# Issuing the zero fills behind the weight loads, with one wait on the output weight

## The chip, the cores and the metric

One Trainium2 chip, one of its cores. The metric is the time of one execution on the device, in microseconds (us). Of the core's engines, PE multiplies matrices, DVE and ACT work on vectors, and SP, ACT and POOL issue DMAs, the copies between memories that 16 DMA engines carry out. "Chain of compute" means the operations that wait for one another from the first load to the last store; a DMA "lands" when its completion is signalled. Executions fall into groups: most take about 766.7 us, others about 783 or 800 us. An execution more than 1.5% above the fastest of its kernel is called slow here, the rest fast.

## The reference

It is one decode step of attention with a feed-forward gate, forward and backward. What matters here is the outputs' size. The caches of keys and values have 2 batches, 8 heads, 32,768 positions and 128 channels, but attention only sees the last 4,096 positions:

```python
W = min(4096, max(256, Sk // 4))                     # 4096 of Sk = 32768
k = jnp.repeat(k_cache[:, :, Sk - W:, :], rep, axis=1)
v = jnp.repeat(v_cache[:, :, Sk - W:, :], rep, axis=1)
...
_out, _vjp = jax.vjp(_f, A_x, A_k_cache, A_v_cache, A_wq, ...)
_grads = _vjp(grad_out)                              # gradients of both whole caches
```

So the gradients of both caches are whole caches (`out_2`, `out_3`), zero in the first 28,672 positions of each of 2 × 16 parts. One part's zeros are 7.34 MB, all of them 235 MB. The rest is small in bytes: weights, 33.6 MB of cache read, 33.6 MB of gradient written.

## The kernel before

The zeros are written from one small tile, by DMAs that POOL issues (`zf`). A "row" is the stretch of bytes that a DMA moves in one piece, for the zeros as it stands in the output. Five parts are cut into several DMAs. The others go out as one DMA each, with rows of 28,672 bytes, or of 57,344 bytes for the 13 parts listed in `zlong`:

```python
def zf(o, q, r0, nent, rows, rep=1):
    ...
    w = rows * DH
    if w > ZG * DH:                  # ZG = 112: a row of 112 * 128 bf16 is 28,672 bytes
        v = v.bitcast(F32)           # 14,336 x f32: 57,344 bytes
        w //= 2
    ...
    sw_fill.append(nc.gpsimd.dma_start(out=v, in_=zs))

zlong = (3, 5, 7, 11, 12, 16, 17, 18, 19, 22, 23, 24, 28)
zshort = {2: (...), 4: (...), 6: (...), 8: (...), 10: (...)}
for qi in range(ZQ - 1):                       # 31 parts, 47 DMAs, right at the start
    r = 0
    whole = (P, ZR // P, 1) if qi in zlong else (P, ZG, ZR // (P * ZG))
    for n, rows, rep in zshort.get(qi, (whole,)):
        r = zf(*zparts[qi], r, n, rows, rep)
```

Further down come the loads. The small ones are issued by ACT, the weights and caches by SP. The LayerNorm and all that follows it need `b2` first in this program's order, then `w1`, `w2`, then `wo`:

```python
dma_store.dma_start(out=b2_bf[:], in_=B_b2...)       # ACT's queue, 1 KB
dma_load.dma_start(out=w1, ...)                      # SP's queue, 1.8 MB
dma_load.dma_start(out=w2, ...)                      # 1.8 MB
dma_load.dma_start(out=wo[:], ...)                   # 4.2 MB
dma_load.dma_start(out=wq[:], ...)                   # 4.2 MB
vnat = load(A_v_cache, 0, "v")                       # 4.2 MB
... # LayerNorm, feed-forward, transposes of wo, w1, w2
knat = load(A_k_cache, 0, "k")                       # reuses the buffer of w1 and w2
... # four rounds of attention: load, compute, store 4.2 MB each of keys and values
... # epilogue
last = nc.sync.dma_start(out=out_6..., in_=dw1_st[:])
with tc.issue_after(last.ins):
    fin = nc.sync.dma_start(out=v, in_=zs)           # zeros of the 32nd part, last of SP
tc.add_manual_dep(fin.ins, sw_fill[-2].ins.name, ...)   # once POOL's second-to-last zero DMA has landed
... # gradient of wo, its store
```

## Time and profile before

| | before |
|---|---|
| time, median of the first 6 runs | 766.78 us (fast runs 766.68 to 766.83) |
| bytes moved | 326.73 MB |
| profiled run | slow: span 797.6 us |
| `wo` lands after its issue | 37.5 us |
| `b2` (1 KB) lands after its issue | 31.2 us |

The page divides the span into 40 equal slices. In the DMA line each digit is the busy share of the 16 DMA engines in tenths, 9 meaning 90% or more; under it stands what they moved. From the page of the kernel before (a slow run: its end is not typical):

```profile
DMA  9999999999999999999999999999999999994089
GB/s 355 437 425 426 436 429 436 421 440 417 434 431 429 433 442 416 434 429 433 434 435 437 429 420 430 432 437 443 422 423 434 434 445 417 429 436 179 1 368 394
```

The engines are busy in all slices but two near the end. Slices 2 to 36 average 431 GB/s, and 326.73 MB at 431 GB/s are 758 us: the fast time of 766.7 us is little more than the bytes. The Trainium skill, "HBM Reference", section "Specifications (TRN2)", gives about 425 GB/s for a core that streams alone, bounded by its 16 DMA engines; this trace agrees, with 431 GB/s.

The timeline of the kernel before shows the start. Columns: start, duration, engine, line, operation, count, and in brackets the idle time before it and what ended it.

```profile
1.64 0.50 SPq L227 DMA_DIRECT2D wo<-in_A_wo_dram  x1
...
4.92 5.20 POOL L101 DMA_DIRECT2D out_dram<-zt  x8 [3.26 <-DVE zt L81]
...
33.20 0.17 DVE L242 CAST b2T<-b_bf 128x4 f32<-128x4 bf16 x1 [18.51 <-DMA b_bf<-in_B_b_dram]
...
33.49 1.87 PE L162 MATMUL pp<-xT_f,ones_f 128*128 128x2 f32 x8 [24.56 <-DVE goT L238]
...
43.68 0.61 POOL L101 DMA_DIRECT2D out_dram<-zt  x1 [33.57 <-DMA out_dram<-zt]
```

POOL issues eight zero DMAs at once, and the ninth at 43.68 us, when the first has landed: at most eight are in flight, called the ring below. The first LayerNorm matmul waits for a copy that stands behind the copy of `b2`, which comes at 33.2 us.

In windows (length, then busy time of PE, weight load, DVE, ACT and POOL, then granted clock, DMA share and GB/s), the first 10 us are the other stretch below the plateau:

```profile
0.00:5.00 5.00, 0.29 (x4) 0.20 (x4) 3.39 (x4) 1.28 (x1) 1.16 (x9) 1.00 0.62 213
5.00:10.00 5.00, 0.26 (x4) 0.28 (x4) 3.24 (x10) 0.00 (x0) 5.00 (x8) 1.00 1.02 345
...
39.00:46.00 7.00, 4.76 (x82) 4.55 (x83) 1.84 (x5) 0.71 (x1) 0.61 (x1) 1.00 1.01 430
```

The issues of the kernel before, with the median time to landing in the last column. In the key and value lines it is not a median of four: asked load by load, the profile gives a landing for the third value load alone, and for the second and fourth key loads.

```profile
nat<-in_A_v_cache_dram SPq DMA_DIRECT2D x4, 4096.0 KB, 33.3
nat<-in_A_k_cache_dram SPq DMA_DIRECT2D x4, 4096.0 KB, 38.7
...
wo<-in_A_wo_dram SPq DMA_DIRECT2D x1, 4096.0 KB, 37.5
```

### The profile page before, as it was taken

The numbers are of one execution on the slowest core, as the hardware profiler recorded it, in microseconds if no ns is written. First come the engines' busy times: TensorE is split into PE (matmuls) and PEld (weight loads), VectorE is DVE, ScalarE is ACT, GpSimd is POOL, SyncE is SP. The second block draws the span as 40 slices with busy tenths as digits, with TensorE's granted clock in tenths as the row PEclk, the third lists the DMA queues.
The fourth block names the chain that finished last, engine by engine and source line by source line (L and its number), as shares of the span: only waits on it lengthen the run. The fifth ranks groups of instructions, "written<-read, shape, count | busy, mean of one in ns | idle before, by whom it ended". The sixth has DMA issues, their size and how long they took to land.

```text
span 797.6 us, 9402 instructions
## 1 busy us (share of the span) xinstructions
PE 412.2 (52%) x4118; PEld 268.4 (34%) x4118; DVE 276.8 (35%) x484; ACT 214.8 (27%) x313; POOL 30.2 (4%) x56
## 2 busy tenths in 40 slices
PE   0265772747503757760573578102608587275690
PEld 0253362634103645420353443002507343134230
DVE  3034241355401436440141375100304555113770
ACT  0024531145400234550120256100202456120260
POOL 3000000010000100000000000000000000000000
PEclk9998897868756995675595968655958577556555
DMA  9999999999999999999999999999999999994089
GB/s 355 437 425 426 436 429 436 421 440 417 434 431 429 433 442 416 434 429 433 434 435 437 429 420 430 432 437 443 422 423 434 434 445 417 429 436 179 1 368 394
DMA packets 12473, 326.73 MB, mean 410 GB/s; under 512 B 2276, under 2 KB 2284, under 8 KB 2294
## 3 DMA queue, kind: packets, MB, share of 16 engines
q0 software_dynamic: 8000, 227.55, 67.5%
q1 hardware_dynamic: 2696, 56.63, 20.3%
q10 hardware_dynamic: 1736, 41.95, 12.4%
q8 instruction: 32, 0.52, 0.2%
q14 instruction: 9, 0.07, 0.0%
HBM read 45.62 MB, written 280.50 MB: 409 GB/s over the span
## 4 chain that ended last, share of the span: by engine, by line
DMA 38%; PE 31%; DVE 14%; ACT 7%; issue 4%; another core or an unknown queue 3%; ACTq 0%; DVEq 0%; SPq 0%
DMA out_dram<-nat 14%; DMA nat<-in_A_k_cache_dram 10%; DMA nat<-in_A_v_cache_dram 9%; PE ov L410 5%; PE tp L377 4%; PE s_ps L383 4%; DMA b_bf<-in_B_b_dram 4%; DVE tT L156 3%; PE dp_ps L383 2%; DVE ds_bf L457 2%; ACT p_bf L444 2%; DVE nat L156 2%; PE wps L628 2%; ACT tT L154 2%
## 5 line engine op out<-in xcount | busy, mean ns | idle before, releaser
L377 PE MATMUL tp<-pperm,nat 128*128 128x128 bf16 x1024 | 84.8, 234 | 177.7 <-DMA nat<-in_A_v_cache_dram 123.6
L156 DVE COPY tT<-tp 128x1024 bf16<-128x1024 bf16 x96 | 64.0, 689 | 244.1 <-PE tp L377 243.7
L377 PEld LDWEIGHTS <-nat 128*128 128x128 bf16 x1024 | 74.0, 106 | 184.1 <-DMA nat<-in_A_v_cache_dram 125.3
L154 ACT COPY tT<-tp 128x1024 bf16<-128x1024 bf16 x32 | 32.4, 1012 | 307.2 <-PE tp L377 307.2
L154 ACT CAST nat<-ov 128x512 bf16<-128x512 f32 x160 | 87.9, 589 | 58.3 <-PE ov L410 57.0
L156 DVE CAST nat<-ov 128x512 bf16<-128x512 f32 x96 | 65.3, 690 | 54.0 <-PE ov L410 53.0
L410 PE MATMUL ov<-bd,ds_bf 128*128 128x512 bf16 x128 | 50.6, 473 | 5.9 <-DVE nat L156 3.9
L410 PE MATMUL ov<-bd,p_bf 128*128 128x512 bf16 x128 | 48.7, 449 | 4.6 <-DVE nat L156 1.8
L383 PE MATMUL dp_ps<-tT,zdo 128*128 128x256 bf16 x256 | 41.1, 293 | 15.2 <-DVE tT L156 8.9
L101 POOL DMA_DIRECT2D out_dram<-zt x47 | 28.6, 613 | 524.3 <-DMA out_dram<-zt 521.0
L383 PE MATMUL s_ps<-tT,zq 128*128 128x256 bf16 x256 | 39.4, 280 | 14.8 <-DVE tT L156 8.8
L383 PEld LDWEIGHTS <-zdo 128*128 128x128 bf16 x256 | 25.5, 104 | 23.3 <-issue 19.9
L399 PE MATMUL ps<-t,nat 128*128 128x16 bf16 x1024 | 28.5, 173 | 7.8 <-DVE bd L367 7.8
L399 PEld LDWEIGHTS <-nat 128*128 128x128 bf16 x1024 | 28.5, 103 | 11.0 <-issue 5.8
L383 PEld LDWEIGHTS <-zq 128*128 128x128 bf16 x256 | 24.8, 100 | 22.0 <-issue 19.5
L495 PE MATMUL wps<-dq_rows,xn_bf 2*128 2x512 bf16 x32 | 14.5, 521 | 22.9 <-ACT wq L154 17.7
L391 PE MATMUL tp<-ident_bf,p_bf 128*128 128x128 bf16 x64 | 7.5, 311 | 34.9 <-ACT p_bf L444 34.9
L444 ACT ACTIVATE p_bf<-e_sb,rl 32x512 bf16<-32x512 f32 x16 | 22.8, 1424 | 3.4 <-DVE rl L441 3.2
L457 DVE SCALAR_TENSOR_TENSOR ds_bf<-dp_ps,delta,p_bf 32x512 bf16<-32x512 f32 x16 | 21.7, 1354 | 0.2
L156 DVE CAST wq<-wps 128x512 bf16<-128x512 f32 x16 | 11.0, 690 | 30.5 <-PE wps L495 30.1
L154 ACT CAST dw_st<-wps 128x512 bf16<-128x512 f32 x15 | 8.8, 586 | 46.6 <-PE wps L608 43.8
L410 PEld LDWEIGHTS <-ds_bf 128*128 128x128 bf16 x128 | 13.6, 113 | 22.8 <-issue 20.2
(197 smaller groups left out, 452.7 us busy)
## 6 DMA issues: line engine op xcount, KB each, us to landing
out_dram<-zt POOLq DMA_DIRECT2D x26, 7168.0 KB, 163.1
out_dram<-nat ACTq DMA_DIRECT2D x8, 4096.0 KB, 31.7
nat<-in_A_v_cache_dram SPq DMA_DIRECT2D x4, 4096.0 KB, 33.3
nat<-in_A_k_cache_dram SPq DMA_DIRECT2D x4, 4096.0 KB, 38.7
out_dram<-zt POOLq DMA_DIRECT2D x4, 3584.0 KB, 56.5
out_dram<-zt SPq DMA_DIRECT2D x1, 7168.0 KB, 31.1
out_dram<-zt POOLq DMA_DIRECT2D x1, 6120.0 KB, 85.9
wo<-in_A_wo_dram SPq DMA_DIRECT2D x1, 4096.0 KB, 37.5
```

Of the source, the lines that this page charges most:

```text
L101: sw_fill.append(nc.gpsimd.dma_start(out=v, in_=zs))
L154: nc.scalar.copy(out=out_ap, in_=in_ap)
L156: nc.vector.tensor_copy(out=out_ap, in_=in_ap)
L377: nc.tensor.transpose(tp[:, j, :], nat[:, g * CC + half * CH + j, :], pperm[:].rearrange("p b k -> p (b k)"))
L383: nc.tensor.matmul(out_ps[:, half * CH * PB:(half + 1) * CH * PB], lhsT=zbuf[:, pr, o:o + R], rhs=tT[:, :, pr, :], start=(g == 0 and pr == ...
L391: nc.tensor.transpose(tp[:, cc, :], src[:, half * CH + cc].rearrange("r k b -> r (k b)"), ident_bf[:, :])
L399: nc.tensor.matmul(ps[:], lhsT=nat[:, g * CC + half * CH + cc, :], rhs=cols[half][:, cc, :, g, :], start=(half == 0 and g == 0 and cc == 0 ...
L410: nc.tensor.matmul(ov[:], lhsT=src[:, cc].rearrange("r k b -> r (k b)"), rhs=bd[:, gh * 4:(gh + 1) * 4, :], start=True, stop=True)
L444: nc.scalar.activation(out=p_bf[rb, :, :, pr], in_=e_sb[rb], func=ACT.Copy, scale=rl[rb, 0:1])
L457: nc.vector.scalar_tensor_tensor(out=ds_bf[rb, :, :, pr], in0=dp_c[rb], scalar=delta[rb, 0:1], in1=p_bf[rb, :, :, pr], op0=ALU.subtract, o ...
L495: nc.tensor.matmul(wps[:], lhsT=xn_bf[:, k:D:DK], rhs=dq_rows[:, :], start=True, stop=True)
L628: nc.tensor.matmul(wps[:], lhsT=o_rows[:, j:N:NJ], rhs=ds_rows[:, :], start=True, stop=True)
```

## The change

The intent is to let the weights load undisturbed, so that the chain of compute starts sooner. The zero DMAs move behind the loads in the source, and the first of them waits until `wo` has landed. All others stand behind it in POOL's queue.

```diff
-    for qi in range(ZQ - 1):
-        ...  r = zf(*zparts[qi], r, n, rows, rep)  ...
 ...
-        dma_load.dma_start(out=wo[:], in_=A_wo.rearrange("(p j) m -> p j m", j=NJ))
+        wo_in = dma_load.dma_start(out=wo[:], in_=A_wo.rearrange("(p j) m -> p j m", j=NJ))
         dma_load.dma_start(out=wq[:], in_=A_wq.rearrange("(p k) n -> p k n", k=DK))
         vnat = load(A_v_cache, 0, "v")
+        for qi in range(ZQ - 1):
+            ...  r = zf(*zparts[qi], r, n, rows, rep)  ...
+        tc.add_manual_dep(sw_fill[0].ins, wo_in.ins.name,
+                          mybir.DependencyInfo(mybir.DependencyClass.Sync, mybir.DependencyReason.DATA))
```

More of the change, by code (lines that the diff above doesn't have):

```diff
@@ L114 @@
     }
-    for qi in range(ZQ - 1):
-        r = 0
-        whole = (P, ZR // P, 1) if qi in zlong else (P, ZG, ZR // (P * ZG))
-        for n, rows, rep in zshort.get(qi, (whole,)):
-            r = zf(*zparts[qi], r, n, rows, rep)
-        assert r == ZR
     eps_t = const.tile([P, 1], F32, name="eps_t")
@@ L226 @@
         dma_load.dma_start(out=w2, in_=B_w2.rearrange("(p j) d -> p j d", j=FK))
-        dma_load.dma_start(out=wo[:], in_=A_wo.rearrange("(p j) m -> p j m", j=NJ))
+        wo_in = dma_load.dma_start(out=wo[:], in_=A_wo.rearrange("(p j) m -> p j m", j=NJ))
         dma_load.dma_start(out=wq[:], in_=A_wq.rearrange("(p k) n -> p k n", k=DK))
         vnat = load(A_v_cache, 0, "v")
+        for qi in range(ZQ - 1):
+            r = 0
+            whole = (P, ZR // P, 1) if qi in zlong else (P, ZG, ZR // (P * ZG))
+            for n, rows, rep in zshort.get(qi, (whole,)):
+                r = zf(*zparts[qi], r, n, rows, rep)
+            assert r == ZR
+        tc.add_manual_dep(sw_fill[0].ins, wo_in.ins.name,
+                          mybir.DependencyInfo(mybir.DependencyClass.Sync, mybir.DependencyReason.DATA))
         tp = ps_m.tile([P, DK, B], BF16, tag="m")
```

## The prediction

> **What bounds the kernel.** Bytes. The DMA line of the page is 9 tenths or more in 37 of 40 slices; slices 2 to 36 move 431 GB/s on average. 326.73 MB at that rate is an estimated 758 us, against fast runs of 766.7 to 766.8. The other 9 us is mostly the start (213 and 345 GB/s in the first two 5 us windows: about 3.5 us lost) and the last completion. The profiled execution is a slow one (797.6 us, clock 0.72): there the DMAs idle from about 727 to 757 us while PE, at a granted clock of 0.50, works off the epilogue. The fast runs leave no room for that gap; I put it at 0 to 3 us.
>
> **What the change intends.** The output weight (issued at 1.6 us) lands 37.5 us later, at 39.1, because zeros share the engines. Without zeros, the 7.86 MB of w1, w2 and wo would take an estimated 20 us at 420 GB/s, and the startup chain (the chain of waits begins with b2's 1 KB load, 31.2 us, then the LayerNorm at 33.5) would begin up to 20 us earlier. As no byte goes away, only the tail gap could be saved.
>
> **What it really does.** The order of instructions shows the two programs alike on PE, DVE, ACT and SP; on POOL one thing differs. The scheduler has put the zero DMA of the second cache part (7.3 MB, waiting only for the memset) ahead of that of the first, and the wait for wo's load sits on the latter, the second instruction. So one zero DMA of 7.3 MB still goes out at 4.9 us. It is just the one that fills the loading time: in the trace the first zero DMA lands at about 43.5 us (the ninth issue, which waits for it, starts at 43.68), later than wo. Until then its ring has work in both kernels: the Trainium skill, "DMA: Bandwidth & Descriptors", section "Queues, rings and completion order", says that each engine takes packets in turn from the queues that have work, and in ring order within one. The trace agrees: 15.3 MB moved by 39.1 us, about half of it the three weights. So b2, w1, w2 and wo should land when they did. Then the seven held issues go out (5.2 us for eight in the trace) while the rest of the first zeros and the queued wq and value loads (8.4 MB) keep the engines busy.
>
> **Predicted:** 766.7 us in the fast state, 8 in 10 between 765.0 and 769.0 (a median that catches three slow runs would lie above). Faster by over 2%: 0.02; within 2%: 0.96; slower by over 2%: 0.02. Even had the wait held the first DMA, I would have expected within 1% in the fast state.
>
> **What would show it.** Right: first POOL issue still near 4.9 us, alone, the next seven near 39 to 45 us; b2 lands near 33 us, wo near 39; the first LayerNorm matmul near 33.5; DMA share 9 or more through the first 60 us; GB/s of slices 2 to 36 near 431. Wrong: b2 or wo landing, or the value or key load starting, over 5 us earlier, or a dip of GB/s between 39 and 46 us.
>
> **What would make it wrong.** Engines that finish their share of the first zeros well before wo lands would give wq a head start and pull the chain a few us: in a slow run, where the tail gap is 30 us, that counts fully, in a fast run hardly. A larger fast-state gap than I estimate would make any shift visible. A lower rate of loads alone than the 418 GB/s of the mix could cost 1 to 2 us.

## The result, and the profile after

The time is 766.76 us (median of 10 runs, 7 of them fast), beside 766.83 us (20 runs of the kernel before). The ratio of the fast runs is 0.9999, with a 95% interval from 0.9989 to 1.0009: the same. Ratios here are the mean time of one kernel's fast runs over that of the other's fast runs of the same rounds, so not quite the ratio of the medians quoted.

The profiled run of the changed kernel is a fast one, span 764.8 us. Its page:

```profile
DMA  9999999999999999999999999999999999999998
GB/s 360 429 429 427 440 418 433 437 429 422 429 432 436 428 432 428 434 421 438 435 430 439 433 436 417 430 433 429 447 432 430 418 433 432 441 422 427 426 427 369
```

There is no idle slice at the end, as I had estimated for fast runs; slices 2 to 36 average 431 GB/s again. The start of its timeline:

```profile
1.64 0.50 SPq L220 DMA_DIRECT2D wo<-in_A_wo_dram  x1
...
4.91 0.84 POOL L101 DMA_DIRECT2D out_dram<-zt  x1 [3.26 <-DVE zt L81]
...
32.99 0.17 DVE L243 CAST b2T<-b_bf 128x4 f32<-128x4 bf16 x1 [18.51 <-DMA b_bf<-in_B_b_dram]
...
33.28 1.87 PE L155 MATMUL pp<-xT_f,ones_f 128*128 128x2 f32 x8 [24.36 <-DVE goT L239]
...
39.44 4.96 POOL L101 DMA_DIRECT2D out_dram<-zt  x8 [33.68 <-DMA wo<-in_A_wo_dram]
```

This is the whole result. One zero DMA still goes out at 4.91 us, and it is alone. The rest follow at 39.44 us, released by `wo`. (Eight are shown in that row: the seven held ones and the ninth, for which nothing was left to wait.) `b2` and the first LayerNorm matmul come 0.2 us earlier than before, and `wo` lands after the same 37.5 us. The windows and the issues answer line by line to those of before (the key and value lines set a fast run beside a slow one, so nothing is read from their difference):

```profile
0.00:5.00 5.00, 0.29 (x4) 0.21 (x4) 3.39 (x4) 1.28 (x1) 1.16 (x9) 1.00 0.69 213
5.00:10.00 5.00, 0.26 (x4) 0.28 (x4) 3.24 (x10) 0.00 (x0) 0.76 (x1) 1.00 1.00 354
...
39.00:46.00 7.00, 4.82 (x88) 4.62 (x87) 1.83 (x4) 0.49 (x1) 4.96 (x8) 1.00 1.01 430
```

```profile
nat<-in_A_v_cache_dram SPq DMA_DIRECT2D x4, 4096.0 KB, 31.9
nat<-in_A_k_cache_dram SPq DMA_DIRECT2D x4, 4096.0 KB, 35.5
...
wo<-in_A_wo_dram SPq DMA_DIRECT2D x1, 4096.0 KB, 37.5
```

In the 7 us in which the ring of zeros might have run dry (39 to 46 us) both kernels moved 430 GB/s. At the other end, SP issues the last zero DMA at this time (timeline of SP in the changed kernel):

```profile
729.31 0.44 SPq L624 DMA_DIRECT2D out_dram<-zt  x1
```

At 431 GB/s, the 35.5 us from here to the end of the span move 15.3 MB at most. The DMA itself has 7.3 MB, the store of `wo`'s gradient 4.2 MB and that of `w1`'s gradient 1.8 MB, 13.4 MB together. So hardly anything else is left to move at 729 us. I read it so that the chain of compute is just in time: the kernel is bound by bytes, but with little slack behind them. The experiments measure it.

### The profile page after: what moved, and what is told of

It is laid out like the page before. It is cut to its first block, busy times and chain, and to the rows that moved or that the text cites. A ratio compares the mean times of both kernels' runs of the same rounds, so it can differ in the third digit from the quotient of the medians.

```text
span 764.8 us, 9402 instructions
## 1 busy us (share of the span) xinstructions
PE 411.0 (54%) x4118; PEld 268.1 (35%) x4118; DVE 277.0 (36%) x484; ACT 214.7 (28%) x313; POOL 30.2 (4%) x56
## 4 chain that ended last, share of the span: by engine, by line
DMA 39%; PE 31%; DVE 15%; ACT 8%; issue 4%; ACTq 0%; DVEq 0%; SPq 0%
DMA nat<-in_A_k_cache_dram 18%; DMA out_dram<-nat 17%; PE ov L411 7%; PE s_ps L384 4%; DMA b_bf<-in_B_b_dram 4%; PE tp L378 3%; DVE nat L149 3%; DVE ds_bf L458 2%; ACT p_bf L445 2%; ACT nat L147 2%; DVE tT L149 2%; PE wps L629 2%; PE ps L400 2%; PE dops L309 1%; PE sps L516 1%
## 5 line engine op out<-in xcount | busy, mean ns | idle before, releaser
L411 PE MATMUL ov<-bd,ds_bf 128*128 128x512 bf16 x128 | 48.1, 453 | 5.9 <-DVE nat L149 4.1
L384 PE MATMUL s_ps<-tT,zq 128*128 128x256 bf16 x256 | 40.0, 283 | 12.6 <-DVE tT L149 8.8
L496 PE MATMUL wps<-dq_rows,xn_bf 2*128 2x512 bf16 x32 | 14.7, 529 | 24.9 <-ACT wq L147 19.7
## 6 DMA issues: line engine op xcount, KB each, us to landing
nat<-in_A_v_cache_dram SPq DMA_DIRECT2D x4, 4096.0 KB, 31.9
nat<-in_A_k_cache_dram SPq DMA_DIRECT2D x4, 4096.0 KB, 35.5
wo<-in_A_wo_dram SPq DMA_DIRECT2D x1, 4096.0 KB, 37.5
```

What stands on the lines that cost most here:

```text
L384: nc.tensor.matmul(out_ps[:, half * CH * PB:(half + 1) * CH * PB], lhsT=zbuf[:, pr, o:o + R], rhs=tT[:, :, pr, :], start=(g == 0 and pr == ...
L411: nc.tensor.matmul(ov[:], lhsT=src[:, cc].rearrange("r k b -> r (k b)"), rhs=bd[:, gh * 4:(gh + 1) * 4, :], start=True, stop=True)
L496: nc.tensor.matmul(wps[:], lhsT=xn_bf[:, k:D:DK], rhs=dq_rows[:, :], start=True, stop=True)
```

## The experiments

Theory: (1) the added wait holds the second zero DMA only, and the one in front of it is as long as the loading of the weights, so nothing changes; (2) even a wait that holds them all would not change the fast time, because bytes bound it. The rival says that the startup chain is on the critical path, so that a wait that really holds saves up to 20 us.

### The move without the wait

```diff
-        tc.add_manual_dep(sw_fill[0].ins, wo_in.ins.name, ...)
```

> The moved zero DMAs without the added wait. The built program is that of the kernel before on every engine, the first cache part's zeros in front again: 766.7 us in the fast state, first zero issue near 4.9 us with seven behind it, wo near 39 us. If the place in the source mattered by itself, a difference would show here.

The built program has the same order and the same waits as the kernel before on every engine, first part in front. (Built again, the changed kernel differs from it in two instructions alone, the first two zero DMAs: they have changed places, and the second waits for `wo`.) So it is the dependency, not the move, that made the scheduler swap the first two. Its first look was a slow run, like two of the three others; the one fast run took 766.83 us. In the slow profile the first eight zero DMAs go out at 4.91 us, the ninth at 43.61, and `wo` lands after 37.3 us. Three slow runs of four say nothing about this program, since it is the same program.

### Every zero DMA held

The wait is put on the first zero DMA as soon as it is made, and all later ones get an order edge behind it, so that none can be scheduled in front:

```diff
+        with ExitStack() as order:
             for qi in range(ZQ - 1):
                 ...
                     r = zf(*zparts[qi], r, n, rows, rep)
+                    if len(sw_fill) == 1:
+                        tc.add_manual_dep(sw_fill[0].ins, wo_in.ins.name, ...)
+                        order.enter_context(tc.issue_after(sw_fill[0].ins))
-        tc.add_manual_dep(sw_fill[0].ins, wo_in.ins.name, ...)
```

> Every zero DMA held until the output weight wo has landed; nothing reaches the engines from the zero ring before. My theory (the change as built leaves a 7.3 MB zero DMA in front; the fast state is bound by bytes): b2 lands before 16 us instead of 33, wo near 21 us instead of 39, first LayerNorm matmul before 16 us, first key load issued near 87 us instead of 106, PE done near 723 us instead of 743, and still 766.7 us within 1.5 us in the fast state. Rival A (a wait that really holds makes the kernel faster, because the startup chain is on the critical path): 747 us. Rival B (it does not matter which zero is held, the loads land when they did): wo still near 39 us.

It took 766.00 us (6 runs, 765.78 to 766.24). Ratio of fast runs 0.9992, interval 0.9976 to 1.0008. Run again:

> The same program as the one that holds every zero until wo has landed, again, for a tighter interval: 766.0 us, 0.6 us below the fast runs of the kernel before (ratio 0.9992), and few or no slow runs, since its chain has about 8 us more before it leaves the DMA engines idle.

It took 765.98 us (5 runs, 765.84 to 766.24), ratio 0.9991, interval 0.9979 to 1.0004. So two jobs give the same 0.7 us less, each with an interval that includes no difference. The timeline:

```profile
1.66 0.48 SPq L220 DMA_DIRECT2D wo<-in_A_wo_dram  x1
...
20.41 0.17 DVE L246 CAST b2T<-b_bf 128x4 f32<-128x4 bf16 x1 [8.93 <-DMA b_bf<-in_B_b_dram]
...
20.70 1.87 PE L155 MATMUL pp<-xT_f,ones_f 128*128 128x2 f32 x8 [11.78 <-DVE goT L242]
...
22.93 5.20 POOL L101 DMA_DIRECT2D out_dram<-zt  x8 [21.29 <-DVE meanb L156]
```

and its issue of `wo`:

```profile
wo<-in_A_wo_dram SPq DMA_DIRECT2D x1, 4096.0 KB, 20.6
```

Now the first weights load really undisturbed. `wo` lands after 20.6 us instead of 37.5, `b2`'s copy comes at 20.41 us instead of 32.99, the first matmul at 20.7 us instead of 33.3, and POOL's first zero DMA only at 22.93 us. (The row names DVE as the releaser because that event came last before it; what the built program waits for there is `wo` and the memset.) My numbers for the start were too hopeful: I had expected `b2` before 16 us and the key load at 87 us; it was issued at 95.0 us (106.3 in the changed kernel). But the chain did start 12.6 us earlier, and the time did not follow. The page:

```profile
GB/s 381 422 428 428 453 414 425 441 431 424 425 431 435 427 443 429 422 430 434 425 433 433 443 433 413 434 433 429 442 429 435 422 432 431 438 422 429 425 439 358
```

The 0.7 us are about the gain of the first slice: 381 GB/s for 19.1 us is 0.40 MB more than 360 GB/s, or 0.9 us. That is a comparison of two traces and no test. The last zero DMA of SP, first and second look:

```profile
721.49 0.46 SPq L627 DMA_DIRECT2D out_dram<-zt  x1
```

```profile
712.30 0.39 SPq L627 DMA_DIRECT2D out_dram<-zt  x1
```

It is issued 7.8 and 17.0 us earlier than in the changed kernel. In the second look this DMA was itself held back, by the wait for POOL's second-to-last zero DMA, which landed at 712.28 us; by the store in front of it (issued at 721.11 and 709.95 us) the two looks differ by 11.2 us in their chain, and by 0.3 us in their span (764.1 and 764.4 us). That is what slack behind the bytes looks like. The rival's 747 us is refuted.

### Loads alone for longer

As above, but waiting for the first value load (`loaded[0]`, the DMA that `load` issues) instead of `wo`.

> Zeros held until the first value load has landed (16.3 MB loaded alone, 40 us). Theory: loads alone move about 420 GB/s, so only the latency between that landing and the first zero bytes is lost, since then nothing else is queued: 767 to 770 us, with one short dip near 40 us. If loads alone run slower than the mix, say 350 GB/s, it costs 8 us: 775 us.

769.67 us (4 runs, 769.09 to 770.11), ratio 1.0039, interval 1.0021 to 1.0056. The windows:

```profile
10.00:39.00 29.00, 12.33 (x154) 11.48 (x155) 6.42 (x26) 2.80 (x4) 0.00 (x0) 1.00 1.01 435
39.00:46.00 7.00, 5.37 (x36) 2.84 (x35) 1.17 (x3) 4.16 (x3) 2.17 (x4) 1.00 0.31 131
```

The loads alone move 435 GB/s, no less than the mix, so holding zeros is not paid for in rate. What is paid is the hole between the landing and the first zero bytes, with nothing else queued. From 39 to 46 us only 131 GB/s are moved, which is worth about 4.9 us at 431 GB/s; the time went up by 3.7 us over the kernel that waits for `wo`. Waiting for `wo` costs nothing because `wq` and the values are still queued behind it.

### Zeros held far too long

The block of zero DMAs stands behind the copy of the transposed queries, and the first one waits for that copy.

```diff
-        nc.vector.tensor_copy(out=qT_all[:], in_=tp[:])
+        q_done = nc.vector.tensor_copy(out=qT_all[:], in_=tp[:])
+        ... # the zero DMAs as above, with q_done in place of wo_in
```

> Zeros held far too long, until the transposed queries are ready (estimate 85 us; wo and wq and the first values have landed by about 42 us). Theory that each idle us of the DMA engines costs one us in a kernel bound by bytes: 44 to 48 us idle, so 808 to 816 us. If zeros only fill holes and the chain bounds: 766 us.

812.08 us (4 runs, 811.49 to 812.24), ratio 1.0590. The page:

```profile
DMA  9900799999999999999999999999999999999998
GB/s 384 418 2 1 315 433 427 444 413 443 421 431 440 418 428 431 452 412 436 431 428 434 444 431 433 423 429 429 432 447 426 424 429 431 429 439 421 431 433 356
```

Two slices of 20.3 us stand empty and the fifth lost about a quarter (315 of 430 GB/s, 5.4 us): an estimate of 46 us idle. The time is 46.1 us above that of the kernel that waits for `wo`. Each idle microsecond of the DMA engines cost one microsecond, which is theory (2) seen from the other side.

### Fewer bytes: the last zero DMA of POOL dropped

If bytes bound, fewer bytes must be faster, up to where the chain takes over. This result is wrong (part of one output stays unwritten, as in the runs below that drop a part).

```diff
-    for qi in range(ZQ - 1):
+    for qi in range(ZQ - 2):
```

> The kernel before without the LAST of the zero DMAs that POOL issues (7.3 MB fewer, wrong result on purpose), so that everything up to about 700 us runs as before. Dropping the first one took 801 us: its key and value loads took 42 and 45 us against 32 and 35, so I think it shifted which zero DMA meets which load. If that is so, this one leaves the loads alone and in the fast state the chain bounds it, the last zero DMA still issued near 729 us: 762 to 765 us. If dropping bytes anywhere makes the loads slower: near 800 us. If bytes alone bound: 749.7 us.

Two of the six runs are fast, 762.05 and 763.36 us; four are slow, and so is the profiled one, which is not used. Ratio of fast runs 0.9948, interval 0.9930 to 0.9966. The 7.34 MB are 17.0 us at 431 GB/s; only 3.4 to 4.7 us of it came back. The kernel before thus has about 4 us of slack in its fast state (from two runs, neither of them profiled): take more than that away from the DMA engines, and the chain bounds it.

### The same with every zero DMA held

> Zeros held until wo has landed, and the last zero DMA of POOL dropped (wrong result on purpose). The chain of the held kernel issues its last zero DMA at 721.5 us, 7.8 us earlier than the kernel with the change. If that head start is real slack hidden behind the bytes, this should end about 7.8 us before the kernel that only drops the last one: 754 to 758 us. If the hold buys nothing: no difference.

749.01, 749.01 and 749.27 us, and one run of 760.37; ratio 0.9770, interval 0.9755 to 0.9785. The dropped bytes now come back in full: 766.0 minus 17.0 is 749.0. I had expected 754 to 758, reckoned from a chain that ends like that of the first look; as the second look showed, it can end 11 us sooner. The page of this kernel has no idle slice:

```profile
DMA  9999999999999999999999999999999999999998
```

So the wait that really holds does buy the chain time. Alone it is worth nothing, since the bytes hide it; with the bytes gone, it is worth about 13 us (762.7 in the mean against 749.1).

### Fewer bytes: the first zero DMA dropped

```diff
-    for qi in range(ZQ - 1):
+    for qi in range(1, ZQ - 1):
```

> The kernel before without the zero DMA of the first cache part (7.3 MB fewer, wrong result on purpose). If bytes alone bound the fast state: 17.0 us less (7.34 MB at 431 GB/s), 749.7 us. My theory is that the chain of compute ends only about 3 us ahead of the point where it would bound: in the fast trace the last zero DMA is issued at 729.3 us and the 14.6 MB still to move then are nearly all its own and the last stores. So I expect 762 to 765 us, with a dip in the DMA line before 730 us.

A plain miss: 800.15 to 808.15 us in all four runs, though 7.3 MB fewer are moved. (That all four were slow is a rival that the times alone do not exclude; the packets below bear on it.) Page and issues:

```profile
DMA  9999999999999999999999999999999999550089
GB/s 370 420 436 432 423 442 423 437 419 434 429 431 433 437 427 430 432 446 423 436 434 425 424 433 446 425 427 429 433 432 431 439 424 427 237 235 28 1 364 390
```

```profile
nat<-in_A_v_cache_dram SPq DMA_DIRECT2D x4, 4096.0 KB, 42.2
nat<-in_A_k_cache_dram SPq DMA_DIRECT2D x4, 4096.0 KB, 45.2
```

Four slices near the end are idle or half idle, so the chain bounds. It is late because its value and key loads take longer: the landings are 42.2 us (third value load) and 45.2 us (mean of the second and fourth key loads), against 31.9 and 35.5 us in the changed kernel. With every zero DMA held as well, the same drop behaved as reckoned:

> Zeros held until wo has landed, and 7.3 MB of zeros fewer (wrong result on purpose). My theory: the hold buys the chain about 20 us of slack, worth nothing alone, but now the dropped bytes count in full: 749.7 us within 2 us. If the hold buys no slack: the same as with the bytes dropped alone, 762 to 765 us.

It took 749.19 us (three runs of 748.94 to 749.33, one of 766.05), ratio 0.9771, with value and key loads of 30.9 and 31.8 us. So it is not the missing part. The drop seems to shift which zero DMAs the loads meet, and the hold to shift it back. Two kinds of zero DMA meet the loads: rows of 28 KB and rows of 56 KB. The next runs set the row length for all plain zero DMAs, with the same bytes. (The long rows are also written as 4-byte elements, the short ones as 2-byte, both from a 1-byte tile: length and element size change together here.)

### Row length of the zeros

```diff
-    zlong = (3, 5, 7, 11, 12, 16, 17, 18, 19, 22, 23, 24, 28)
+    zlong = ()                      # all plain zero DMAs in rows of 28 KB
```

> The kernel before with all plain zero DMAs in rows of 28 KB (13 of them had rows of 56 KB). Same bytes. If a longer zero row takes a longer turn at the engine and the loads get a smaller share beside it: key and value loads land in 30 us or less in the median (32 to 39 before), the last zero DMA is issued before 725 us, and still 766.7 us within 1.5 us, bytes bound. If only the order in which zeros and loads meet matters: medians of 32 to 39 us.

767.10 us in all four runs (767.08 to 767.25), ratio 1.0004. Issues, and the last zero DMA of SP:

```profile
nat<-in_A_v_cache_dram SPq DMA_DIRECT2D x4, 4096.0 KB, 30.9
nat<-in_A_k_cache_dram SPq DMA_DIRECT2D x4, 4096.0 KB, 34.2
...
wo<-in_A_wo_dram SPq DMA_DIRECT2D x1, 4096.0 KB, 38.3
```

```profile
718.79 0.43 SPq L623 DMA_DIRECT2D out_dram<-zt  x1
```

```diff
-    zlong = (3, 5, 7, 11, 12, 16, 17, 18, 19, 22, 23, 24, 28)
+    zlong = tuple(range(ZQ))        # all in rows of 56 KB
```

> The opposite: all plain zero DMAs in rows of 56 KB. If row length sets the share of the loads: the startup weights land later too (wo near 50 us instead of 39), key and value loads in 40 us or more, the chain late, DMA engines idle before the end, 795 us or more. If not: 766.7 us, or the spread of the kernel before.

816 to 818 us in three runs and 847.31 in one; ratio 1.0651. Issues:

```profile
nat<-in_A_v_cache_dram SPq DMA_DIRECT2D x4, 4096.0 KB, 41.5
nat<-in_A_k_cache_dram SPq DMA_DIRECT2D x4, 4096.0 KB, 32.8
...
wo<-in_A_wo_dram SPq DMA_DIRECT2D x1, 4096.0 KB, 55.4
```

The cleanest witness is `wo`, since at the start nothing but the zero rows differs: 38.3 us with short rows, 55.4 us with long ones. In these two traces `w2` lands 19.5 and 29.2 us after its issue at 1.2 us. From there `wo`, whose rows are 32 KB, took 19.3 and 26.7 us more. If each engine takes one row of the loads and one of the zeros in turn, the 4.19 MB of `wo` come with 4.19 × 28/32 or 4.19 × 56/32 MB of zeros, and at 430 GB/s that is an estimated 18.3 and 26.8 us. The measured pairs fit. The landings of the later loads fit less well. With long rows the values take 41.5 us but the keys 32.8, where I had expected 40 or more for both; with short rows the keys take 34.2 where I had expected 30. The key figures are means of two unlike loads, 24.6 and 41.0 us with long rows, 28.6 and 39.9 us with short ones. A landing also holds the wait for the completion: of the load with 39.9 us, the last row was in 24.9 us after the issue. The times answer clearly all the same: the same bytes take 50 us more with long rows.

### First zero DMA dropped, all rows short

> The first zero DMA dropped (7.3 MB fewer, wrong result on purpose) from the kernel whose zero rows are all 28 KB. With the mixed rows that drop took the time to 801 us. If the cause there was that 56 KB rows then met the key and value loads, it can't happen here: loads land in 28 to 34 us, and the time is between the 750 us of the bytes and the 754 us of a chain that issues its last zero DMA at 719 us. If dropping the first zero DMA itself upsets the loads: near 800 us.

750.11 to 750.16 us in three runs, 754.21 in the profiled one; ratio 0.9797, loads of 31.9 and 32.1 us. The drop that took the mixed rows to 801 us takes the short rows to the 750 us of the bytes. Long zero rows meeting the loads are thus the cause of that miss.

The traces record every packet of every DMA, and in them each row of the zeros and of the loads is one packet. So it can be followed which rows a load met (from its first row to its last; the first value load, which queues at the start, is left out). Over all 14 traces, 65 key and value loads passed beside 10 long zero rows at most: their last row was in 22 to 32 us after the issue. 16 loads passed beside 100 long rows or more: 33 to 38 us. The other 17 lie between, at 24 to 35 us. In the first two groups the number of zero rows beside a load was much the same, 102 to 162 and 116 to 169, so about one for each of its 128 rows, long or short. In the run with the first zero DMA dropped, the first key load met 72 long rows, the second 161, the third value load 130 and the third key load 106. With every zero DMA held as well, the same four met 42, 0, 0 and 9; with all rows short there are none. Whether the drop alone always leads there, or did so in these four runs, is not shown.

## Why the prediction was right

- **The wait is in the wrong place.** Right. First issue at 4.91 us, alone; the next at 39.44 us; `b2` at 33.0, `wo` at 39.1 and the first matmul at 33.3 us, all as written down.
- **One zero DMA fills the loading time.** Right: `wo` lands after the same 37.5 us with one zero DMA in the ring as with eight, and that one landed at 43.3 us, 4 us after `wo`. That one part of the zeros is just long enough is a chance of its size, which the prediction had read from the trace. The Trainium skill, "DMA: Bandwidth & Descriptors", section "Queues, rings and completion order", has each engine take packets in turn from the queues that have work; then a longer ring behind the same head changes nothing for its neighbours. The trace agrees.
- **Nothing idles at the handover.** Right: 430 GB/s from 39 to 46 us in both.
- **Even a proper wait would stay within 1%.** Right: 766.0 us, with a chain that starts 12.6 us earlier.
- **A tail gap of 0 to 3 us in fast runs.** The fast profile shows no gap; there is slack of about 4 us on the other side.
- **Up to 20 us earlier for the startup chain, were the zeros held.** Too high: 12.6 us at the first matmul. `wo` did land near the estimated 20 us, but the chain begins with `b2`, which took 18.4 us beside the weights alone.

What stays open is what sets off a slow run. What makes it late is in the packets: in the three slow profiles (the kernel before, the move without the wait, the last zero DMA dropped) the last three loads passed beside 102 to 144 long zero rows each, in the fast profile of the changed kernel beside 4, 0 and 54, and SP's last zero DMA goes out near 765 us instead of 729. So the miss at 801 us and the slow runs look like one thing. The granted clock hardly tells the states apart: 0.709 to 0.724 in slow runs of the kernel before, 0.720 to 0.740 in its fast ones, and 0.714 to 0.726 in the held kernel, whose runs were all fast.

The kernel before had 20 slow runs in the 56 timed with these kernels and the changed one 3 in 10. The kernel with every zero DMA held had none in 11 (but one in four with either part dropped), the one with short rows none in 4. That is a count, and why one run meets the long rows and the next does not was not tested. It does make the held version the one I would keep: it is never behind in these runs, and 0.7 us ahead in the fast state, though neither interval excludes no difference.

## What to carry to other kernels

When the DMA engines are busy from end to end, an earlier start of the compute chain is worth only as much as the chain lacks at the end; drop some bytes on purpose to see how much slack there is. A wait on one of several independent instructions holds that one alone: look at the built order before you believe it holds those behind it. And a bulk write of long rows slows the loads beside it more than one of short rows, though both move the same bytes. And ask for the landings one by one before you lean on a median: here "x4" stood over one or two of them.

## What the Trainium skill lacked or had wrong

- "DMA: Bandwidth & Descriptors", section "Queues, rings and completion order": it says that an engine drains a packet, typically 9 to 17 descriptors, before it switches. Here shares follow the row length as if one row went per turn, and in the packet records each row is one packet: beside 28 KB rows `wo` landed after 38.3 us, beside 56 KB rows after 55.4 us. The page does not say that row length decides the share.
- The same page, section "Anatomy of one DMA": about 2 us fixed cost plus bytes over the rate, fitted for DMAs that POOL issues. The 1 KB load of `b2`, which ACT issues (128 rows of 8 bytes), took 18.4 us beside the weights and 31.2 us beside weights and zeros. Each of its packets took 27 ns at most in the kernel before, but they started between 12.0 and 30.6 us, as turns taken row by row would have it. What such a load costs beside bulk traffic is on no page that I found.
- The same page, section "Measured": 425 GB/s for a 16 MB load. The loads alone moved 435 GB/s here, the mix of loads and stores 431 GB/s: the rate agrees, and the mix is on none of its rows. But the row's own size and time, 16 MB in 79.0 us, give 212 GB/s, half of it; so do the other rows.
